# First q and k loads over all partitions from two queues, wider w_in packets, output blocks in score banks and a searched early order, in a fused attention and softplus-MLP kernel

## The chip, the cores and the metric

The kernel runs on one core of one Trainium2 chip. The metric is device microseconds of one execution. The profile also gives a span, from the first to the last instruction; it is some 2 us shorter than the time. Runs more than 1.5% above the fastest of the same kernel are called slow and are left out of all ratios.

The engines are named as in the profile: PE (matmul), PEld (weight load of PE), DVE (vector), ACT (scalar), POOL (GpSimd), SP (sync; it only issues transfers here). ACT issues transfers too, and ACTq and SPq mark the issuing itself.

## The reference, cut to what matters

```python
# q, k, v: (4, 8, 768, 64) f32     w_in: (512, 2048) f32     w_out: (2048, 512) f32
scores = q @ k.T / sqrt(64) - slope[h] * dist          # per batch and head
keep   = (key is one of the first 8) | (0 <= query - key < 96)
a      = softmax(where(keep, scores, -1e9))
x      = (a @ v), heads side by side                    # (4 * 768, 512)
g      = max(x @ w_in, 0) + log1p(exp(-abs(x @ w_in)))  # softplus
out    = g @ w_out                                      # (3072, 512) f32
```

A query needs only its own block of 128 keys, the block before and the 8 global ones. There are 4 sequences of 6 blocks, so 24 blocks of 128 tokens, and 12 groups of two blocks for the MLP. Inputs are f32; the kernel casts them to bf16.

## The kernel before

A planner inside the kernel lists every operation with an engine, a guessed duration and a rank, simulates the engines, and fixes each engine's order of instructions from that. On the chip each engine keeps to its order: an operation whose data are late holds up all that stand behind it.

```python
FIRST_UNITS = [[0], [1], [2, 3]]      # which sequences' first blocks are loaded together
FIRST_LOADS = "u0 u1 u2 i0 i1 i2 i3 i4 i5 i6 i7 o0 u3 o1 o2 o3 o4 o5 o6 o7".split()
FILLERS = 90                          # matmuls on zeros that keep PE busy at the start
O_KEYS = {(0, 1): ("s", 3), (1, 0): ("s", 2)}   # output banks other than "o"
...
s_ps = ps.tile([P, 16, P], F32, name="s_ps")    # ONE tile over four PSUM banks, for scores
x_ps = ps.tile([P, 512], F32, name="x_ps")      # one bank each
h_ps = [ps.tile([P, 512], F32, name=f"h_ps{i}") for i in range(2)]
o_ps = ps.tile([P, 512], F32, name="o_ps")
```

`u` is a unit of q, k and v, `i` an eighth of w_in (512 KB), `o` an eighth of w_out (512 KB). A first block's q comes in two halves, each to 64 partitions, as runs of two rows of 64 floats, which is 512 bytes.

```python
for y in range(2):
    eng = second if y else "SP"
    part = src[s, 4 * y : 4 * y + 4, sl, :]     # four heads, 128 rows
    def fn(part=part, slot=slot, y=y, eng=eng, nh=nh):
        return dma_on[eng].dma_start(
            raw_t[slot][64 * y : 64 * y + 64, 0 : P * nh].rearrange("p (h c) -> p h c", h=nh),
            part.rearrange("h (p r) d -> p h (r d)", r=2),
        )
```

w_in comes as eight column slices, in runs of 256 floats (1 KB); every weight is cast on POOL. q and k of the first blocks are cast and turned by PE into score banks, then copied out. Most output blocks accumulate 16 w_out matmuls in the one bank `o_ps` and are copied out by DVE:

```python
def store(g, ns, rank):
    parts = [(0, DM)] if 2 * g + ns < NIT - 1 else [(0, 256), (256, DM)]
    for a, z in parts:
        def cp(a=a, z=z):
            nc.vector.tensor_copy(osb[:, a:z], bank(key)[:, a:z])
    ...
```

The softmax here doesn't subtract the row's maximum and nothing guards it: scores larger than these inputs give would overflow.

## Time and profile before

| | before |
|---|---|
| time, median of the first 3 runs | 234.69 us (234.14 to 236.62) |
| span, mean granted clock | 232.6 us, 0.989 |
| PE / ACT / DVE / POOL busy | 92 / 67 / 49 / 42% |
| first w_in matmul | 21.17 us |
| third MLP group begins (129th w_in weight load) | 56.6 us |
| last w_in cast begins, last w_out cast begins | 30.3 us, 48.8 us |

The page of the kernel before, its head. The rows under the busy times cut the span into 40 equal slices: the granted PE clock in tenths, the busy share of the 16 DMA engines in tenths, and what they moved. The last line is the head of the chain of waits, as shares of the span.

```profile
span 232.6 us, 5037 instructions
PE 214.6 (92%) x1994; PEld 149.0 (64%) x2026; DVE 113.1 (49%) x219; ACT 154.9 (67%) x202; POOL 98.1 (42%) x178
PEclk9999999999998899999999999999999999999998
DMA  5999999999796449868877545899679422110021
GB/s 156 224 235 350 352 305 375 360 253 223 199 270 168 122 93 239 190 187 216 133 166 163 133 135 119 243 131 242 168 188 176 113 73 68 48 45 36 10 93 45
PE 78%; DMA 7%; DVE 4%; POOL 3%; issue 3%; ACT 3%; DVEq 0%; POOLq 0%; ACTq 0%
```

The windows view of the same kernel: stretch, length, then busy time and count of PE, PEld, DVE, ACT and POOL, the granted clock, the DMA share and GB/s. The share adds up packet times, so it can pass 1.

```profile
4.00:6.00 2.00, 2.00 (x14) 1.44 (x12) 1.69 (x8) 1.64 (x3) 0.00 (x0) 1.00 1.03 275
12.00:14.00 2.00, 0.94 (x12) 0.80 (x12) 0.62 (x2) 0.77 (x2) 0.00 (x0) 1.00 1.22 217
22.00:24.00 2.00, 1.73 (x21) 1.33 (x22) 0.74 (x3) 1.19 (x3) 1.48 (x2) 1.00 1.10 348
```

While q, k and v come, full engines move between 275 GB/s (4 to 6 us) and 217 (12 to 14 us); while w_in comes (22 to 24 us) they move 348.

The timeline of the kernel before: start, length, engine, line, operation, output and input with sizes, count, and in brackets the engine's idle time just before with what ended it. First the start-up, then the last output blocks.

```profile
5.70 0.43 DVE L370 CAST qb<-raw 128x512 bf16<-128x512 f32 x1
19.41 1.04 POOL L350 CAST w_in_bf<-raw 128x1024 bf16<-128x1024 f32 x1
21.17 1.05 PE L657 MATMUL h_ps<-XT,w_in_bf 128*128 128x256 bf16 x8
...
220.75 3.61 PE L704 MATMUL o_ps<-w_out_bf,g 128*128 128x512 bf16 x16 [0.78 <-DVE osb L728]
225.15 3.61 PE L704 MATMUL o_ps<-w_out_bf,g 128*128 128x512 bf16 x16 [0.78 <-DVE osb L728]
```

The first 21 us hold no MLP work. At the end PE stands still for 0.78 us before each of the last two output blocks, because the one bank has to be copied out first.

How far the needed work has come is read by counting the weight loads in the trace: every w_in and every w_out matmul has one, 768 and 384 in all. By the durations in the chain of waits (eight w_in matmuls 0.87 us, four w_out matmuls 0.86 us), one w_in load stands for 0.109 us of needed PE time and one w_out load for 0.215 us. All "needed work" below is an estimate from these two.

### The profile page before, as it was taken

Reading aid. Unit: us, or ns where it says so; the run is one execution under the profiler, and the core shown is the slowest. Engines: PE = TensorE matmul, PEld = TensorE weight load, DVE = VectorE, ACT = ScalarE, POOL = GpSimd, SP = SyncE. Lnnn points to the kernel's source line nnn. Section 1 sums busy time; section 2 is a strip of 40 time slices with the busy share of each in tenths; the row PEclk is TensorE's granted clock in tenths of the full one; section 3 lists DMA queues with packets and bytes.
Section 4 is the critical chain, followed back from the end, with each engine's and each line's share of the span. In section 5 each row is a group of like instructions: output and inputs, shape, how many; then the busy total and the mean of one; then the engine's idle time right before and its main releaser. Section 6 shows DMA issues by size and latency. Waiting matters only on the chain.

```text
span 232.6 us, 5037 instructions
## 1 busy us (share of the span) xinstructions
PE 214.6 (92%) x1994; PEld 149.0 (64%) x2026; DVE 113.1 (49%) x219; ACT 154.9 (67%) x202; POOL 98.1 (42%) x178
## 2 busy tenths in 40 slices
PE   8979889898995998999999999999999999999883
PEld 5758777555753476777667667676766867667531
DVE  5567315474179494059538448732944862111111
ACT  2432977751985259898878959876885987676600
POOL 3437645789456224767701606341573630000000
PEclk9999999999998899999999999999999999999998
DMA  5999999999796449868877545899679422110021
GB/s 156 224 235 350 352 305 375 360 253 223 199 270 168 122 93 239 190 187 216 133 166 163 133 135 119 243 131 242 168 188 176 113 73 68 48 45 36 10 93 45
DMA packets 76872, 40.97 MB, mean 176 GB/s; under 512 B 30640, under 2 KB 71856, under 8 KB 76848
## 3 DMA queue, kind: packets, MB, share of 16 engines
q1 hardware_dynamic: 75216, 39.86, 68.2%
q10 hardware_dynamic: 1632, 0.79, 1.4%
q8 instruction: 16, 0.26, 0.5%
q14 instruction: 8, 0.07, 0.1%
HBM read 27.26 MB, written 6.29 MB: 144 GB/s over the span
## 4 chain that ended last, share of the span: by engine, by line
PE 78%; DMA 7%; DVE 4%; POOL 3%; issue 3%; ACT 3%; DVEq 0%; POOLq 0%; ACTq 0%
PE o_ps L704 30%; PE h_ps L657 29%; PE s_ps L546 5%; PE h_ps L807 5%; DMA raw<-in_k_dram 4%; PE s_ps L704 3%; DMA raw<-in_v_dram 3%; PE x_ps L601 2%; ACT pb L581 2%; PE x_ps L598 2%; DVE z L572 2%; POOL vb L501 2%; POOL vb L395 1%; DVE osb L728 1%; PE s_ps L443 1%
## 5 line engine op out<-in xcount | busy, mean ns | idle before, releaser
L657 PE MATMUL h_ps<-XT,w_in_bf 128*128 128x256 bf16 x768 | 95.5, 273 | 1.5 <-POOL w_in_bf L350 0.9
L704 PE MATMUL o_ps<-w_out_bf,g 128*128 128x512 bf16 x323 | 84.8, 385 | 4.0 <-DVE osb L728 1.6
L657 PEld LDWEIGHTS <-w_in_bf 128*128 128x128 bf16 x768 | 73.2, 98 | 20.2 <-POOL w_in_bf L350 2.2
L672 ACT ACTIVATE e<-h_ps 128x512 f32<-128x512 f32 x96 | 59.9, 630 | 30.9 <-PE h_ps L657 30.3
L704 PEld LDWEIGHTS <-g 128*128 128x128 bf16 x384 | 35.9, 99 | 36.2 <-issue 7.0
L572 DVE TENSOR_TENSOR z<-s_ps,biasA 128x1024 f32<-128x1024 f32 x40 | 48.1, 1218 | 18.7 <-PE s_ps L546 17.0
L581 ACT ACTIVATE pb<-z 128x1024 bf16<-128x1024 f32 x40 | 41.8, 1050 | 18.9 <-DVE z L572 18.8
L683 ACT ACTIVATE g<-e 128x1024 bf16<-128x1024 f32 x48 | 50.7, 1056 | 1.3
L395 POOL CAST vb<-raw 64x512 bf16<-64x512 f32 (+1 forms) x60 | 32.8, 547 | 23.1 <-DMA raw<-in_v_dram 17.5
L728 DVE COPY osb<-o_ps 128x512 f32<-128x512 f32 (+1 forms) x23 | 15.2, 665 | 51.4 <-PE o_ps L704 51.3
L395 POOL CAST kb<-raw 64x512 bf16<-64x512 f32 (+1 forms) x44 | 24.0, 545 | 17.5 <-DMA raw<-in_k_dram 15.9
L501 POOL COPY vb<-vb 4x512 bf16<-4x512 bf16 x32 | 19.5, 610 | 17.1 <-PE x_ps L601 16.0
L611 DVE TENSOR_TENSOR xs<-x_ps,rcp 128x256 bf16<-128x256 f32 x46 | 19.5, 424 | 1.6
L610 DVE RECIPROCAL rcp<-x_ps 128x4 f32<-128x4 f32 x46 | 8.3, 179 | 22.8 <-PE x_ps L601 19.5
L601 PE MATMUL x_ps<-vb,pb 128*128 128x65 bf16 x160 | 15.1, 194 | 1.6 <-POOL vb L501 1.5
L598 PE MATMUL x_ps<-vb,pb 128*128 128x65 bf16 x160 | 15.5, 194 | 0.7 <-ACT g L683 0.7
L598 PEld LDWEIGHTS <-pb 128*128 128x128 bf16 x160 | 12.5, 98 | 5.2 <-issue 1.9
L492 POOL COPY kT<-kTf 128x32 bf16<-128x32 bf16 x16 | 3.5, 217 | 27.9 <-PE s_ps L546 27.0
L807 PE MATMUL h_ps<-blank 128*128 128x256 bf16 x90 | 13.8, 305 | 1.2 <-POOL blank L751 1.1
L546 PE MATMUL s_ps<-qT,kT 64*128 64x128 bf16 x288 | 13.4, 217 | 0.7 <-DVE z L572 0.7
L601 PEld LDWEIGHTS <-pb 128*128 128x128 bf16 x160 | 11.3, 97 | 3.4 <-issue 1.0
L370 DVE CAST qb<-raw 128x1024 bf16<-128x1024 f32 (+1 forms) x15 | 9.6, 641 | 7.5 <-DMA raw<-in_q_dram 7.5
(49 smaller groups left out, 98.6 us busy)
## 6 DMA issues: line engine op xcount, KB each, us to landing
out_dram<-osb SPq DMA_DIRECT2D x23, 256.0 KB, 2.4
raw<-in_moe_w_in_dram SPq DMA_DIRECT2D x8, 512.0 KB, 9.5
raw<-in_moe_w_out_dram SPq DMA_DIRECT2D x8, 512.0 KB, 8.3
raw<-in_q_dram SPq DMA_DIRECT2D x8, 512.0 KB, 4.3
raw<-in_k_dram SPq DMA_DIRECT2D x8, 512.0 KB, 5.5
raw<-in_v_dram SPq DMA_DIRECT2D x8, 512.0 KB, 4.9
raw<-in_q_dram SPq DMA_DIRECT2D x10, 128.0 KB, 3.5
raw<-in_k_dram SPq DMA_DIRECT2D x10, 128.0 KB, 3.6
```

The costliest lines, as they stand in the source:

```text
L395: copy_on[eng](dst, src[64 * x : 64 * x + 64, r, :, :])
L501: nc.gpsimd.tensor_copy(vb_of(prev)[sl, :, 0:D], vb_of(first)[sl, :, 0:D])
L546: nc.tensor.matmul(s_ps[:, reg, :].rearrange("p (r t) -> p r t", r=2), kt[rows, m, :], qv(rows, m), start=not biased, stop=True, skip_grou ...
L572: nc.vector.tensor_tensor(z[:, 0:nr, :], src, bias, ALU.add)
L581: nc.scalar.activation(pb[:, 0:nr, :], src, AF.Exp, scale=1.0 / root_d)
L598: nc.tensor.matmul(xv[:, m, :], pb[:, 2 * m, :], vb_of(n)[:, h, :], start=True, stop=False)
L601: nc.tensor.matmul(xv[:, m, :], pb[:, 2 * m + 1, :], vb_of(prev)[:, h, :], start=False, stop=True)
L657: last = nc.tensor.matmul(hv[:, j, :], w_in_bf[:, m, fb * P : fb * P + P], XT[g % NXG][:, m, :], start=(m == 0), stop=(m == NM - 1),)
L672: nc.scalar.activation(e[:, p % 2, :, :].rearrange("p j (b t r) -> p (j b) r t", b=2, r=2), hb[:].rearrange("p (a r t) -> p a r t", a=4, r=2),
L683: nc.scalar.activation(gt[:, 2 * p - 2 : 2 * p + 2, :].rearrange("p a t -> p (a t)"), e[:].rearrange("p a j t -> p (a j t)"), AF.Ln, bias=1.0,
L704: nc.tensor.matmul(bank(key), gt[:, fb, ns * P : ns * P + P], w_out_bf[:, fb, :], start=(fb == 0), stop=(fb == NFB - 1),)
L807: nc.tensor.matmul(h_ps[0][:, 0:256], blank[:, 0:P], blank[:])
```

## The change

The intent: get the first q and k sooner, start the MLP sooner, and shorten the tail.

```diff
-FIRST_UNITS = [[0], [1], [2, 3]]
-FIRST_LOADS = "u0 u1 u2 i0 i1 i2 i3 i4 i5 i6 i7 o0 u3 o1 o2 o3 o4 o5 o6 o7".split()
+FIRST_UNITS = [[0, 1], [2, 3]]
+FIRST_LOADS = "k0 q0 v0 q1 k1 i3 i1 i0 i2 v1 i7 i4 i5 i6 k2 o0 q2 o1 v2 o5 o7 o4 o2 o6 o3".split()
+ACT_LOADS = "q0 q1 k1 v0 k0".split()
+LEADS = {3: 1.75, 4: 2.5, 5: 2.5, 6: 2.5, 7: 3.25, 8: 2.75, ...}
+RANK = {0: -4, 1: -4, 2: -12, 3: 0, 4: 12, 5: 990, 6: -12, ...}
-O_KEYS = {(0, 1): ("s", 3), (1, 0): ("s", 2)}
+O_KEYS = {(0, 1): ("s", 3), (1, 0): ("s", 2),
+          (10, 0): ("s", 0), (10, 1): ("s", 1), (11, 0): ("s", 2), (11, 1): ("s", 3)}
+NARROW = (0, 1, 2)     # quarters of w_in that still come in 1 KB runs; the last comes in 2 KB runs
+ENG = {...}            # casts and copies of the first units on POOL, ACT, DVE
+ENG_W = {"i0": "POOL", "i1": "ACT", "i2": "POOL", ...}   # weight casts on three engines
...
 # in load_unit, first q and k: four rows of 64 floats are one run of 1 KB
+    for y in range(2):
+        eng = second if y else "SP"
+        c0 = 256 * (len(u) * y + x)
+        def fn(src=src, raw=raw, y=y, eng=eng, s_=s_, c0=c0):
+            return dma_on[eng].dma_start(
+                raw[:, c0 : c0 + 256],
+                src[s_, y::2, sl, :].rearrange("h (p r) d -> h p (r d)", r=4),
+            )
+        work = (0.38, 51.0)      # planned: 0.38 us of the engines for 128 KB
...
 # in store, the last block
-        parts = [(0, DM)] if 2 * g + ns < NIT - 1 else [(0, 256), (256, DM)]
+        parts = [(0, 256, "DVE", "SP"), (256, DM, "ACT", "ACT")] if last else [(0, DM, "DVE", "SP")]
```

Cut: the casts and copies that unpack the new layout, a shorter way to compute the distances, the later start of the second set of biases, and small changes of planned durations.

A first load now takes 4 heads of 32 four-row runs, 128 KB, to 128 partitions (head and run together make the partition). Units 0 and 1 together need 16 such loads for q and k: 2 MB.

## The prediction

> **What bounds the kernel now.** The page gives a span of 232.6 us (clock 0.989), PE 92% busy, but not all of that is needed work. In the chain eight w_in matmuls (128x256) take 0.87 us and four w_out matmuls (128x512) 0.86 us: 768 of the first need 84 us, 384 of the second 82 us; attention about 1.1 us of PE per block, 24 blocks. Needed: some 190 us. Busy times by stretch and line show where the other 40 go:
> - 0 to 21 us: no w_in matmul; PE runs 90 fillers and waits for the first blocks. First q cast at 5.7 us, first w_in cast at 19.4, first w_in matmul at 21.2. DMA moves about 220 GB/s while q, k, v come, 350 once w_in (1 KB runs) flows.
> - 21 to 55 us: each w_in matmul group waits for a weight cast that waits for its transfer (one per 1.5 us). By 55 us PE has done about 131 w_in and 41 w_out weight loads of 768 and 384. The third group begins at about 55 us.
> - 55 to 85 us: lumpy, a 6.7 us wait for v on the chain, the clock at half for 3.4 us near 75 us.
> - 85 to 220 us: PE-bound, needed work near 100%.
> - 220 to 232.6 us: two gaps of 0.78 us (w_out matmuls wait for the copy out of the only output bank), then 3.8 us of copy and store.
>
> **What the change does.** q and k of two first blocks at a time come in 1 KB runs over 128 partitions from two queues; by these rates 512 KB take 1.5 us instead of 2.3. (The Trainium skill, "DMA: Bandwidth & Descriptors", Specifications, puts line rate at 512 B and more; this trace differs, 220 against 350 GB/s, though start-up is in the 220.) w_in comes before v of the second pair. Only the last quarter of w_in uses 2 KB runs: worth 0.3 us. Weight casts spread from POOL (1.04 us each) over DVE, ACT and POOL; the first biases leave ACT (1.7 us).  The last four output blocks get score banks, and the last copy is split over DVE and ACT.
>
> **Cost on the critical path**, estimated from those durations:
> - The first 2.6 MB land by about 12 us, so the first w_in matmul comes at 16 to 17 us instead of 21.2; the last w_in lands at 26 instead of 30 us, all w_out at 42 instead of 48.
> - The third group starts at about 47 us instead of 55, with the first two groups' w_out work nearly done rather than two thirds (23 matmuls, 5 us). Together 13 us.
> - 55 to 85 us: 3 us of waits and low clock.
> - Tail: 2 x 0.78 plus about 0.4: 2 us.
> - Steady state: nothing.
> Sum 18 to 19 us: time about 216 us, range 208 to 226. Faster by over 2% 0.94, within 2% 0.05, slower 0.01.
>
> **What shows it right or wrong.** First w_in matmul at 16 to 17 us, first w_in cast near 14; DMA near 300 GB/s from 3 us on; third group's w_in matmuls by 47 us; output copies no longer release PE after 200 us; matmul counts per us from 100 to 200 us as before. Clock 0.99 or above.
>
> **What would make it wrong.** The order is fixed by a planner; a transfer later than planned blocks all behind it on its engine (ACT now has v casts ahead of its exponentials), and the 13 us shrink. The interleaved q layout gives PE strided operands: perhaps a microsecond or two. And 1 KB runs may be no faster when two queues share the engines.

## The result, and the profile after

| | before | changed |
|---|---|---|
| time, median of 4 runs | 234.84 us (234.14 to 236.62) | 247.08 us (244.89 to 248.29) |
| span, clock (profiled run) | 232.6 us, 0.989 | 245.2 us, 0.965 |
| first w_in matmul | 21.17 us | 38.85 us |
| 129th w_in weight load | 56.6 us | 74.7 us |

The ratio is 1.050, with a 95% interval of 1.041 to 1.059: slower by 5%, where 8% faster had been predicted. A ratio here is the mean time of one kernel's fast runs over that of the other's of the same rounds, so it is not quite the ratio of the medians.

The page of the changed kernel, the same lines:

```profile
span 245.2 us, 5044 instructions
PE 219.5 (90%) x1995; PEld 151.3 (62%) x2026; DVE 114.9 (47%) x219; ACT 159.5 (65%) x210; POOL 90.1 (37%) x166
PEclk9988756999999999999999999999999999999999
DMA  1527879999796876999992974479942761200112
GB/s 51 151 92 212 223 204 312 330 371 338 194 208 190 197 155 189 246 218 228 213 177 67 222 190 105 131 186 267 262 81 46 193 110 43 65 14 31 43 45 86
PE 69%; DMA 17%; DVE 7%; issue 2%; POOL 2%; ACT 1%; ACTq 1%; DVEq 0%
```

DMA has gone from 7 to 17% of the chain. In the third slice, where the kernel before has full DMA engines and 235 GB/s, this one has a share of 0.2 and 92 GB/s. The windows view of the changed kernel, in the order of its columns above:

```profile
4.00:6.00 2.00, 2.00 (x12) 1.36 (x10) 0.55 (x4) 0.00 (x0) 1.79 (x4) 1.00 0.27 93
14.00:16.00 2.00, 0.00 (x0) 0.00 (x0) 0.00 (x0) 0.00 (x0) 0.00 (x0) 1.00 0.28 88
15.00:40.00 25.00, 14.61 (x115) 10.06 (x117) 6.34 (x21) 9.13 (x17) 7.75 (x10) 0.68 0.74 206
30.00:35.00 5.00, 2.43 (x23) 1.75 (x20) 0.87 (x4) 1.67 (x3) 1.04 (x1) 0.50 0.61 157
```

From 14 to 16 us no compute engine does anything at all, and the transfers run at 88 GB/s with the engines a quarter busy. The longest pieces of the chain of waits of the changed kernel (start, length, what) say what the program waited for:

```profile
2.45 10.83 DMA raw<-in_q_dram
13.30 4.91 DMA raw<-in_q_dram
18.23 13.85 DMA raw<-in_k_dram
```

These three pieces alone are 29.6 us of loads of the first q and k. The timeline of the changed kernel, the start-up and the tail:

```profile
10.38 1.04 POOL L427 CAST kb<-raw 128x1024 bf16<-128x1024 f32 x1 [4.19 <-DMA raw<-in_k_dram]
25.12 1.04 POOL L427 CAST qb<-raw 128x1024 bf16<-128x1024 f32 x1 [6.78 <-DMA raw<-in_q_dram]
31.55 1.04 POOL L406 CAST w_in_bf<-raw 128x1024 bf16<-128x1024 f32 x1 [5.39 <-DMA raw<-in_moe_w_in_dram]
38.85 1.89 PE L742 MATMUL h_ps<-XT,w_in_bf 128*128 128x256 bf16 x8
...
230.13 3.61 PE L789 MATMUL s_ps<-w_out_bf,g 128*128 128x512 bf16 x15 [0.78 <-DVE osb L814]
234.53 3.61 PE L789 MATMUL s_ps<-w_out_bf,g 128*128 128x512 bf16 x16 [0.78 <-DVE osb L814]
238.93 2.75 PE L789 MATMUL s_ps<-w_out_bf,g 128*128 128x512 bf16 x12 [0.78 <-DVE osb L814]
241.72 0.42 DVE L814 COPY osb<-s_ps 128x256 f32<-128x256 f32 x1 [2.84 <-PE s_ps L789]
242.17 0.37 ACT L814 COPY osb<-s_ps 128x256 f32<-128x256 f32 x1 [12.79 <-DVE osb L814]
```

Two surprises. The casts of the first q and k wait for their transfers, the last of q until 25.12 us and the last of k, on ACT, until 32.23 us. And the tail, meant to lose its gaps, has three of 0.78 us instead of two, though each of the last four blocks has a bank of its own; the last ACT copy waits until the DVE copy beside it is done.

Weight loads done, w_in / w_out, counted in the four traces (sixteen-engines and split-tail are experiments below):

| by | before | changed | sixteen-engines | split-tail |
|---|---|---|---|---|
| 31 us | 56 / 0 | 0 / 0 | 40 / 0 | 45 / 0 |
| 55 us | 128 / 40 | 88 / 6 | 128 / 34 | 128 / 41 |
| 100 us | 287 / 112 | 228 / 92 | 304 / 118 | 306 / 120 |
| 200 us | 683 / 304 | 631 / 280 | 688 / 312 | 703 / 316 |

By 55 us the changed kernel is behind by 40 w_in and 34 w_out loads: 40 x 0.109 + 34 x 0.215, an estimated 11.7 us. By 200 us it is behind by 52 and 24, an estimated 10.8 us. So the loss is made in the start-up and kept; the spans differ by 12.6 us, and the third gap adds 0.8.

### The profile page after: what moved, and what is told of

It is laid out like the page before. It is cut to its first block, busy times and chain, and to the rows that moved or that the text cites. A ratio compares the mean times of both kernels' runs of the same rounds, so it can differ in the third digit from the quotient of the medians.

```text
span 245.2 us, 5044 instructions
## 1 busy us (share of the span) xinstructions
PE 219.5 (90%) x1995; PEld 151.3 (62%) x2026; DVE 114.9 (47%) x219; ACT 159.5 (65%) x210; POOL 90.1 (37%) x166
## 4 chain that ended last, share of the span: by engine, by line
PE 69%; DMA 17%; DVE 7%; issue 2%; POOL 2%; ACT 1%; ACTq 1%; DVEq 0%
PE h_ps L742 30%; PE o_ps L789 21%; DMA raw<-in_q_dram 9%; PE s_ps L789 9%; DMA raw<-in_k_dram 6%; PE s_ps L628 4%; DMA kT<-kb 2%; DVE z L657 2%; PE x_ps L683 2%; PE x_ps L686 2%; DVE osb L814 1%; DVE xs L696 1%; POOL kb L468 1%; ACT pb L666 1%; DVE w_out_bf L406 1%
## 5 line engine op out<-in xcount | busy, mean ns | idle before, releaser
L742 PE MATMUL h_ps<-XT,w_in_bf 128*128 128x256 bf16 x768 | 97.3, 274 | 0.5 <-DVE rcp L695 0.4
L789 PE MATMUL o_ps<-w_out_bf,g 128*128 128x512 bf16 x263 | 69.7, 379 | 1.3
L468 POOL CAST vb<-raw 64x512 bf16<-64x512 f32 (+1 forms) x50 | 27.6, 552 | 8.7 <-DMA raw<-in_v_dram 6.7
L583 POOL COPY vb<-vb 4x512 bf16<-4x512 bf16 x32 | 20.3, 633 | 20.6 <-PE x_ps L686 19.6
L789 PE MATMUL s_ps<-w_out_bf,g 128*128 128x512 bf16 x92 | 22.8, 379 | 4.1 <-DVE osb L814 2.9
L814 DVE COPY osb<-o_ps 128x512 f32<-128x512 f32 x18 | 12.4, 688 | 28.0 <-PE o_ps L789 28.0
L891 PE MATMUL h_ps<-blank 128*128 128x256 bf16 x90 | 15.8, 342 | 1.1 <-POOL blank L836 1.1
L683 PEld LDWEIGHTS <-pb 128*128 128x128 bf16 x160 | 12.6, 98 | 3.1
L814 DVE COPY osb<-s_ps 128x512 f32<-128x512 f32 (+1 forms) x6 | 3.9, 647 | 22.2 <-PE s_ps L789 22.2
L891 PEld LDWEIGHTS <-blank 128*128 128x128 bf16 x90 | 10.5, 121 | 6.1 <-issue 1.9
```

The costliest lines, as they stand in the source:

```text
L468: copy_on[eng](dst, raw)
L583: nc.gpsimd.tensor_copy(vb_of(prev)[sl, :, 0:D], vb_of(first)[sl, :, 0:D])
L683: nc.tensor.matmul(xv[:, m, :], pb[:, 2 * m, :], vb_of(n)[:, h, :], start=True, stop=False)
L742: last = nc.tensor.matmul(hv[:, j, :], w_in_bf[:, m, fb * P : fb * P + P], XT[g % NXG][:, m, :], start=(m == 0), stop=(m == NM - 1),)
L789: nc.tensor.matmul(bank(key), gt[:, fb, ns * P : ns * P + P], w_out_bf[:, fb, :], start=(fb == 0), stop=(fb == NFB - 1),)
L891: nc.tensor.matmul(h_ps[0][:, 0:256], blank[:, 0:P], blank[:])
```

## The experiments

**The theory.** The new source is written with the heads outermost, `h p (r d)`, and there are four heads in a load. The Trainium skill, "DMA: Bandwidth & Descriptors", section "Why a DMA increments its semaphore by 16 and not by 1", says that the number of engines of a transfer is the largest number up to 16 that divides the size of the slowest dimension (other than 1) of both access patterns. With 4 outermost on one side and 128 on the other that is 4 of 16 engines. The trace agrees: the share stands at 0.27 from 4 to 6 us, though by 4.2 us both queues had issued eight of these loads, 1 MB, and the last of them landed at 13.28 us; it is 0.28 from 14 to 16 us. I had not looked this section up for the prediction.

**The rivals.** First, that two queues hamper each other, which the prediction named as its risk. Second, that the granted clock, 0.50 from 30 to 35 us, is the cause and not a consequence. Third, later, that 1 KB runs matter at all.

### Sixteen engines

The row runs go outermost, so that partition p holds run p//4 of head p%4, and the unpacking follows. All else is as in the changed kernel.

```diff
-  src[s_, y::2, sl, :].rearrange("h (p r) d -> h p (r d)", r=4),
+  src[s_, y::2, sl, :].rearrange("h (p r) d -> p h (r d)", r=4),
...
-  v6 = t[:, 4 * x : 4 * x + 4, :].rearrange("p (a r) (m g) -> p m r g a", r=2, m=NPAIR)
+  v6 = t[:, 4 * x : 4 * x + 4, :].rearrange("p (a r) (g m) -> p m r g a", r=2, m=NPAIR)
...
-  cols = tr[:, 4 * x : 4 * x + 4, :].rearrange("p (a r) (m g) -> p r m g a", r=2, m=NPAIR)[:, r]
+  cols = tr[:, 4 * x : 4 * x + 4, :].rearrange("p (a r) (g m) -> p r m g a", r=2, m=NPAIR)[:, r]
```

> The changed kernel with one thing altered: each 128 KB load of the first q and k lists its 1 KB runs row group by row group (outermost source dimension 32) instead of head by head (outermost 4). Same bytes, same run size, same queues, same order on every engine. Theory (each of these loads ran on 4 of the 16 DMA engines): DMA share in the first 4 to 6 us goes from 0.27 to about 1.0 and 93 GB/s to 300 or more, the first w_in matmul comes at 16 to 18 us instead of 38.9, the granted clock stays above 0.98, time 214 to 221 us. Rival A (1 KB runs from two queues get in each other's way) and rival B (the searched order with strict engine queues is what blocks): both say no change, 244 to 248 us.

Measured: 232.35 us (231.19 to 233.74), ratio to before 0.993 (0.984 to 1.002); the result is correct. Against the changed kernel's 247.08 us that is 14.7 us gained by exchanging two dimensions (and by nothing else, as the unpacking does the same work). The windows view of this kernel:

```profile
4.00:6.00 2.00, 2.00 (x13) 1.48 (x11) 0.54 (x3) 0.74 (x1) 1.79 (x4) 1.00 0.87 242
```

The share is 0.87 in place of 0.27, and 242 GB/s in place of 93. First w_in matmul at 24.07 us in place of 38.85. What follows: the loads were the loss. But the kernel is then only level with before: the 214 to 221 us expected were missed, as was the matmul at 16 to 18 us, so the gain that was predicted is still missing.

### Eight engines

The source has all 8 heads outermost and half the rows. It fetches other rows than the casts expect, so its values are wrong; size, run length and queues are the same. (The comparison with the reference nevertheless passed, so that check is blind to this kind of mix-up and proves little for it.)

```diff
-  src[s_, y::2, sl, :].rearrange("h (p r) d -> h p (r d)", r=4),
+  src[s_, :, 64 * y : 64 * y + 64, :].rearrange("h (p r) d -> h p (r d)", r=4),
```

> Wrong result on purpose: the same bytes of the first q and k in 1 KB runs, but each load takes all 8 heads of half the rows, so the outermost source dimension is 8. Theory: 8 of 16 engines, DMA share about 0.5 to 0.55 and 180 GB/s while only q and k flow, first w_in matmul at 22 to 25 us, time 222 to 230 us, between the other two. Rivals A and B: as the changed kernel, 244 to 248 us.

Measured: 236.74 us (235.3 to 241.89, of which the last was a slow run and is left out of the ratio), ratio 1.010 (1.000 to 1.019); first w_in matmul at 27.6 us. Both lie between the other two kernels, as the theory wants, but above the 222 to 230 and 22 to 25 us expected. The windows view of this kernel:

```profile
4.00:6.00 2.00, 2.00 (x18) 1.60 (x16) 0.14 (x2) 0.00 (x0) 1.58 (x3) 1.00 0.51 175
```

With 4, 8 and 32 outermost (4, 8 and 16 engines by the rule) the share goes 0.27, 0.51, 0.87. The 2 MB of q and k would take, as an estimate from the measured rates, 22.5 us at 93 GB/s, 12.0 us at 175 and 8.7 us at 242. The steps between these, 10.5 and 3.3 us, stand beside the steps between the medians, 10.3 (247.08 to 236.74) and 4.4 us (236.74 to 232.35). So the number of engines alone accounts for the loss of the changed kernel.

### Warm clock

Every filler matmul of the changed kernel is done three times, to hold the clock up while PE waits.

```diff
-            nc.tensor.matmul(h_ps[0][:, 0:256], blank[:, 0:P], blank[:])
+            for _ in range(3):
+                nc.tensor.matmul(h_ps[0][:, 0:256], blank[:, 0:P], blank[:])
```

> The changed kernel with each filler matmul issued three times, so that PE stays busy and its clock full while it waits. Rival C (the half clock up to 40 us is the main loss): 232 to 238 us. Theory of the few engines: the clock goes above 0.98 but q still lands at 16 us and the first w_in matmul stays at 36 us or later; gain 1 to 4 us, time 243 to 246 us.

Measured: 250.89 us (250.35 to 251.35), ratio 1.072 (1.064 to 1.080). The windows view of this kernel:

```profile
15.00:40.00 25.00, 22.81 (x237) 19.43 (x236) 5.76 (x16) 8.09 (x14) 8.29 (x11) 1.00 0.74 209
```

The clock is 1.00 where the changed kernel had 0.68, at the same DMA rate (209 against 206 GB/s), and the time is worse, and worse than both expectations. So a full clock doesn't win the loss back. What the low clock cost by itself this run can't show, because the added fillers got in the way: up to 45 us they make up 68.5% of the chain of waits, the first transposes of k begin at 18.18 us instead of 11.47, and the first w_in matmul comes at 41.4 us instead of 38.85. That the low clock was a consequence is shown by the sixteen-engine kernel: with no filler added, its granted clock was 1.00. The Trainium skill, "TensorE: Matmul & The Clock Gate", section "Part 1: The HAM clock gate", has PE at half rate after an idle window of some 3.4 us. The trace of the changed kernel agrees: after PE had stood still for 3.97 us (to 17.16) the clock was 0.50 from 18 to 20 us, and after 3.23 us (to 26.21) it was 0.50 from 28 to 40 us; in the warm-clock kernel, with PE kept busy, it was 1.00.

### One queue

The sixteen-engine kernel, with all its first loads issued by SP.

```diff
-ACT_LOADS = "q0 q1 k1 v0 k0".split()
+ACT_LOADS = []
```

> As e1_sixteen, but all first loads are issued from the SP queue alone (the plan shifts with it). Rival A: faster than e1_sixteen by 2 us or more. Theory: the two queues only save issue time; each issue takes about 0.65 us for 128 KB on one queue, about 200 GB/s, so first w_in matmul 4 to 6 us later than in e1_sixteen and 3 to 6 us slower in time.

Measured: 236.19 us (235.06 to 237.58), ratio 1.011 (1.002 to 1.021): 3.8 us slower than with two queues. The first w_in matmul came at 25.7 us, 1.6 us later, where 4 to 6 us had been expected. The windows view of this kernel, then its timeline of issues:

```profile
4.00:6.00 2.00, 2.00 (x14) 1.52 (x12) 0.14 (x2) 0.00 (x0) 1.74 (x4) 1.00 0.67 190
0.72 2.59 SPq L368 DMA_DIRECT2D raw<-in_k_dram  x4
```

Four issues take 2.59 us, 0.65 us each. At 128 KB an issue, one queue can ask for no more than an estimated 202 GB/s, and 190 were moved. The rival that two queues are in each other's way is false: with one queue the rate falls, because the issuing is then the limit. How much of the 3.8 us is that isn't shown, since the plan shifts with the queues, and a shifted plan alone can move as much (see the replanned kernel below). The Trainium skill, "DMA: Bandwidth & Descriptors", section "Issuing engines are not separate DMA queues", says that issuing from several engines saves only the sequencer's time, "which is usually small relative to the DMA itself". The kind of saving agrees; for 128 KB loads it was not small here.

### Score banks as two tiles

This and the next two ran together. The sixteen-engine kernel's timeline has a strange order at the first scores:

```profile
14.35 0.60 ACT L666 ACTIVATE pb<-s_ps 128x512 bf16<-128x512 f32 x1
15.00 0.61 PE L522 MATMUL s_ps<-ident,qb 128*128 128x128 bf16 x8 [0.31 <-ACT pb L666]
15.64 0.60 ACT L666 ACTIVATE pb<-s_ps 128x512 bf16<-128x512 f32 x1 [0.69 <-PE s_ps L522]
```

PE's transposes wait for an exponential, and the next exponential waits for the transposes, though they use different banks of `s_ps`. The theory: waits are placed for a whole tile, not for a bank. The rival: some true dependence on data. In the experiment the four banks become two tiles of two banks, with nothing else changed:

```diff
-    s_ps = ps.tile([P, 16, P], F32, name="s_ps")
+    s_ab = [ps.tile([P, 8, P], F32, name=f"s_ps{i}") for i in range(2)]
+    def s_reg(r0, nr):
+        return s_ab[r0 // 8][:, r0 % 8 : r0 % 8 + nr, :]
...  # every s_ps[:, a:b, :] becomes s_reg(a, b - a)
```

> e1_sixteen with the four score banks declared as two tiles of two banks instead of one tile of four; same plan, same order. In the e1_sixteen trace the second exponential of the first block (0.60 us at 15.64) waits for the transposes of the next q, which write other banks, and these had waited for the first exponential. Theory D (waits are placed per tile, so banks that the plan thinks free are not): these waits go, the first w_in matmul comes at 20 to 22 us instead of 24.1, time 224 to 229 us. Rival E (what is left of the missing gain is the transfers alone, 250 GB/s for the first 14 us and few transfers in flight): first w_in matmul within 1 us of 24.1, time 230 to 234 us.

Measured: 230.28 us (228.48 to 231.07), ratio 0.981 (0.974 to 0.989); first w_in matmul at 20.9 us in place of 24.07. The timeline of this kernel, at the start and in the tail:

```profile
13.46 1.09 ACT L670 ACTIVATE pb<-s_ps 128x512 bf16<-128x512 f32 x2
14.09 0.61 PE L526 MATMUL s_ps<-ident,qb 128*128 128x128 bf16 x8
212.56 7.07 PE L793 MATMUL s_ps<-w_out_bf,g 128*128 128x512 bf16 x32 [0.78 <-DVE osb L818]
220.41 2.75 PE L793 MATMUL s_ps<-w_out_bf,g 128*128 128x512 bf16 x12 [0.78 <-DVE osb L818]
```

The two exponentials now follow each other at once (x2 in 1.09 us), with the transposes beside them. The first w_in matmul is where the theory wanted it; the time is not, it lies at the edge of what the rival of the transfers foretold (230 to 234 us), and the sixteen-engine kernel ran in another call. In the tail, PE goes from block (10, 1) in bank 1 to block (11, 0) in bank 2, which is another tile, with no gap (x32 in 7.07 us); the block changes inside one tile keep their 0.78 us. The theory holds, and it explains why the changed kernel's tail, where all four blocks are in one tile, had three gaps.

### Kernel before, score banks as two tiles

The same edit on the kernel before.

> The kernel before with the same two tiles and nothing else. Theory D: before pays such waits too, but its plan was weaker, 229 to 233 us. Rival E: 233 to 236 us.

Measured: 234.79 us (233.89 to 235.76), ratio 1.003 (0.994 to 1.011). No gain, where the theory had expected 229 to 233 us. The waits do go here too: in the kernel before the first two exponentials start at 11.57 and 13.17 us, with the split they follow each other from 11.11 us, and the third group begins at 55.2 us instead of 56.6. Why nothing of it is left at the end stays open.

### Split tail

The two-tile kernel, with the last four output blocks in four different tiles.

```diff
     (10, 0): ("s", 0),
-    (10, 1): ("s", 1),
-    (11, 0): ("s", 2),
-    (11, 1): ("s", 3),
+    (10, 1): ("s", 2),
+    (11, 0): ("x",),
+    (11, 1): ("o",),
```

> e7_split with the last four output blocks in four different tiles (two score tiles, x bank, o bank). In the changed kernel PE waits 0.78 us three times near the end for the copy of another bank of the same tile. Theory D: these three gaps go, 2.3 us less than e7_split (1.8 to 2.8). If waits went by bank and the gaps had another cause: no difference from e7_split beyond 0.5 us.

Measured: 227.7 us (227.42 to 228.89), ratio 0.972 (0.966 to 0.979). This version beats both kernels. The timeline of its tail:

```profile
215.04 3.62 PE L793 MATMUL x_ps<-w_out_bf,g 128*128 128x512 bf16 x16
218.49 3.62 PE L793 MATMUL o_ps<-w_out_bf,g 128*128 128x512 bf16 x16
```

No idle time stands before either block. Two gaps of 0.78 us are gone against the two-tile kernel; the medians differ by 2.6 us and the spans of the profiled runs by 1.1 us (226.7 and 225.6), so the 1.6 us of the gaps is within what was seen, and the rest isn't explained (other banks can also shift the plan).

### 512-byte runs

The split-tail kernel with its first q and k in runs of 512 bytes. Rows are mixed up; the bytes and the 16 engines are the same.

```diff
-    raw[:, c0 : c0 + 256],
-    src[s_, y::2, sl, :].rearrange("h (p r) d -> p h (r d)", r=4),
+    raw[:, c0 : c0 + 256].rearrange("p (a c) -> p a c", a=2),
+    src[s_, y::2, sl, :].rearrange("h (p r) d -> p h (r d)", r=2),
```

> Wrong values on purpose: e9_split_tail with the first q and k read in 512-byte runs instead of 1 KB, into the same 128 partitions, on all 16 engines, same order. The step under test is the prediction's '512 KB take 1.5 us instead of 2.3 us' for 2 MB in all, 3.2 us of transfer. If run size is what sets 220 against 350 GB/s: DMA near 220 GB/s from 3 to 10 us, first w_in matmul 2 to 3 us later, time 2 to 3 us more than e9_split_tail. If the start is limited elsewhere (issue, landings of transfers in flight): within 1 us.

Measured: 228.3 us (228.01 to 228.88), ratio 0.974 (0.969 to 0.980). That is 0.6 us above the split-tail kernel. It was run at another time. The windows view of the split-tail kernel and then of this one:

```profile
4.00:6.00 2.00, 2.00 (x16) 1.61 (x14) 0.15 (x2) 0.00 (x0) 1.62 (x5) 1.00 0.92 297
4.00:6.00 2.00, 2.00 (x16) 1.60 (x14) 0.54 (x4) 0.00 (x0) 1.80 (x4) 1.00 0.96 270
```

The rate falls a little, the first w_in matmul comes at 24.2 us instead of 22.0, and almost none of it reaches the end. The run length, on which the prediction had built its first sum, is worth less than 1 us.

### Plain leads and ranks

The split-tail kernel without the searched tables.

```diff
-LEADS = {3: 1.75, 4: 2.5, ...}
-RANK = {0: -4, 1: -4, 2: -12, ...}
+LEADS = {}
+RANK = {}
```

> e9_split_tail with the searched load leads and block ranks taken away (every unit 2.5 groups ahead and every block at its plain rank, as in the kernel before). Between 55 and 100 us the kernel before falls back by another 5 us of needed PE work and e9_split_tail by none. If the searched leads and ranks are what removed that: 3 to 5 us more than e9_split_tail, lost between 55 and 100 us. If it came from the early order or from other moves: within 1.5 us.

Measured: 227.46 us (227.18 to 227.88), ratio 0.971 (0.966 to 0.976). The same time as with the tables: these two parts of the search gained nothing here.

### Replanned with measured transfer times

The planner had 0.38 us for 128 KB, which is 345 GB/s; the traces of the sixteen-engine kernels show less. Here it gets times nearer to the measured ones.

```diff
-    work = (0.38, 51.0)
+    work = (0.48, 51.0)
...
-    work = (0.5, 33.0)
+    work = (0.62, 33.0)
```

> e9_split_tail with the planner told the measured early rates (about 0.48 us for 128 KB of q or k and 0.62 us for 128 KB of v instead of 0.38 and 0.50), so that the fixed order of the engines fits the landings. If the late first w_in matmul (22.0 us in e9_split_tail, 17 us forecast) comes mostly from work queued in strict order behind landings later than planned: first w_in matmul at 19 to 20.5 us and 1 to 3 us less time than e9_split_tail. If the bytes themselves are the limit (7 MB of q, k, v and w_in by 30.9 us in both before and e9_split_tail): within 1 us of e9_split_tail's 227.7.

Measured: 232.55 us (231.65 to 234.82), ratio 0.992 (0.985 to 0.998): 4.9 us worse. The first w_in matmul is unchanged (22.1 us). The chain of waits of this kernel has two long waits for k:

```profile
61.97 5.72 DMA raw<-in_k_dram
103.92 6.46 DMA raw<-in_k_dram
```

They are not the cause by themselves: the chain of the split-tail kernel has two such waits for k as well, 4.59 us from 62.02 and 5.52 us from 97.68. By the counts this kernel is level at 55 us (128 / 43), an estimated 3.4 us behind at 100 us (291 / 112) and 7.4 us at 200 us (667 / 300); its profiled run was the longest of the five. So a truer number for the first loads shifted the planned order long after them, to a worse one; which operations lost the time stays open. A miss on both expectations, and a warning: a change anywhere in the plan can move 5 us.

### First group before the second pair

The split-tail kernel, with the plan pushed to do the first MLP group before the attention of blocks 2 and 3.

```diff
-RANK = {0: -4, 1: -4, 2: -12, 3: 0, ...}
+RANK = {0: -4, 1: -4, 2: 990, 3: 990, ...}
...
-    work = (0.38, 51.0)
+    work = (2.0 if (which, i) in (("k", 1), ("q", 1)) else 0.38, 51.0)
```

> e9_split_tail with the plan made to believe that the second pair's q and k land late, and with the second pair's attention ranked behind the first group's w_in matmuls, so that PE does not stand in line behind k (its cast was at 16.3 us in e9_split_tail) before the transposes that the first group needs. If the first w_in matmul at 22.0 us is set by this line: 19 to 20.5 us and 0.5 to 2 us less time than e9_split_tail's 227.7. If the weights' arrival is what counts (last w_in cast at 30.9 us whatever the order): first w_in matmul may move, time within 1 us.

Measured: 237.66 us (235.67 to 237.88), ratio 1.013 (1.006 to 1.021): worse by 10 us. The first w_in matmul came later (24.6 us) and the third group at 63.9 us. Neither of the two expectations held; why the order is so much worse wasn't followed up.

### Kernel before, tail in two tiles

The kernel before, with the last blocks of the last two groups in `x_ps`.

```diff
-O_KEYS = {(0, 1): ("s", 3), (1, 0): ("s", 2)}
+O_KEYS = {(0, 1): ("s", 3), (1, 0): ("s", 2), (10, 1): ("x",), (11, 1): ("x",)}
```

> The kernel before with nothing changed but that the last four output blocks alternate between the o bank and the free x bank, two tiles. Theory D: the two 0.78 us waits of PE at 220.0 and 224.4 us go, 1.3 to 1.8 us less than the kernel before. If the gap is inherent to a change of block: no difference beyond noise of 0.7 us.

Measured: 234.66 us (233.6 to 236.68), ratio 1.002 (0.995 to 1.010). The timeline of its last two output blocks:

```profile
221.97 3.62 PE L704 MATMUL o_ps<-w_out_bf,g 128*128 128x512 bf16 x16
225.42 3.62 PE L704 MATMUL x_ps<-w_out_bf,g 128*128 128x512 bf16 x16
```

The blocks start 3.45 us apart; in the kernel before it was 4.40 us. So the gaps are gone, and yet the time is the same: by 85 us this kernel had done 192 w_in loads where before had 198, with 96 w_out loads in both. The edit also moved the plan, and the gain was lost to that or to the scatter of the kernel before; which of the two stays open. Inconclusive for the time, clear for the gaps.

## Why the prediction was wrong

Predicted were 216 us (208 to 226) and 0.94 for faster; measured were 247.08 us. Point by point:

- **"q and k of two first blocks at a time come in 1 KB runs over 128 partitions from two queues; by these rates 512 KB take 1.5 us instead of 2.3."** This is the step that failed. The rates were read from transfers that used all engines. The new loads ran on 4 of 16: 93 GB/s, an estimated 5.6 us for 512 KB. I looked at run length and partitions and not at the outermost dimension of the source. It is shown by the 4, 8 and 16 engine runs, and it accounts for the whole loss.
- **"First w_in matmul at 16 to 17 us", third group "at about 47 us", "together 13 us".** Measured: 38.85 and 74.7 us. With all engines at work the matmul comes at 24.07 us, with the tiles split too at 20.9 to 22 us, which is no sooner than before; and the third group at 57.8 us (split-tail) against 56.6 us before. So this part was wrong even without the four engines. The reason is in the bytes: before the last w_in cast can start, 3 MB of q, k and v and 4 MB of w_in must land, in both kernels; that cast starts at 30.3 us before and at 30.87 us in the split-tail kernel (29.2 to 31.8 us in the other two-queue kernels with 16 engines). In the chain of waits of the latter, 10.79 and 8.04 us before that cast are waits for w_in. Reordering loads within the same bytes moved no end, and the average rate did not rise.
- **"This trace differs, 220 against 350 GB/s."** The Trainium skill, "DMA: Bandwidth & Descriptors", section "Specifications", puts line rate at 512 bytes and more. In the kernel before, full engines moved 217 to 275 GB/s in 512-byte runs against 348 in 1 KB runs, but those loads also differ in their partitions and sizes. Where only the run length was changed, it was 270 against 297 GB/s, 1.1 times as fast and not the 1.5 times of the prediction's sum (some loads of v, in short runs in both, lie in that stretch), and less than 1 us of time hung on it.
- **"The last four output blocks get score banks", tail 2 us.** Reading was right that the gaps cost 0.78 us each; wrong was that four banks are four places. They are one tile, and the waits go by tile: three gaps instead of two. In four tiles the gaps go.
- **"The last copy is split over DVE and ACT."** The copies ran one after the other, 241.72 and 242.17 us. Both read one bank, and both write one tile, `osb`. The Trainium skill, "PSUM — Partial Sum Buffer", section "PSUM bank collisions raise a hardware error", counts ScalarE reading beside VectorE in the same bank and quadrant as a collision, to be guarded by bank. The trace agrees that they were kept apart, with 0.03 us between them. Whether the bank or the wait by tile did it isn't separated; that two banks would let them overlap, no run here shows.
- **"55 to 85 us: 3 us of waits and low clock."** Not seen in the changed kernel: from 55 to 100 us it does 140 w_in and 86 w_out loads, 33.8 us of needed work, against 32.8 before. Once the loads are mended the size is about right: 37.2 us in the sixteen-engine kernel and 36.4 in the split-tail one, so about 4 us gained. It doesn't come from the searched leads and ranks (227.46 us without them), and the replanned kernel lost it (32.6). Which part of the new order brings it stays open.
- **"Steady state: nothing."** Right. From 100 to 200 us before does 396 w_in and 192 w_out loads, the changed kernel 403 and 188: 84.4 and 84.3 us of needed work.
- **"Clock 0.99 or above."** It was 0.965; a consequence of the late loads, since the sixteen-engine kernel had 1.00.
- **The named risks.** "A transfer later than planned blocks all behind it" did happen, only far more strongly. "1 KB runs may be no faster when two queues share the engines" did not: one queue alone was 3.8 us slower, in a shifted plan. Strided operands: no run measured them alone.

Where the split-tail kernel's 7.1 us over before come from, as an estimate from the counts: 3.6 us of needed work between 55 and 100 us, 1.0 us between 100 and 200 us (397 and 196 loads, 85.4 us, against 84.4), and 1.6 us of gaps at the end; nothing before 55 us, where 128 / 41 stand against 128 / 40. That is 6.2 us; the rest isn't accounted for.

## What to carry to other kernels

Before costing a transfer by its bytes and run length, look at the size of the outermost dimension of both its sides: a share of the DMA engines that stands at a quarter or a half with loads still queued is a sign that most engines have no part in it (loads issued too slowly lower the share as well, here to 0.67). Before counting on an earlier end of a start-up, look whether fewer bytes stand before its last transfer or the rate rises: here another order of the same 7 MB ended at about the same time. And a bank is free only if the program's waits know it as a thing of its own: give buffers that should overlap separate tiles.

## What the Trainium skill lacked or had wrong

- "DMA: Bandwidth & Descriptors", the number of engines of a transfer: right (4, 8 and 32 outermost, so 4, 8 and 16 engines, gave shares of 0.27, 0.51 and 0.87, and 93, 175 and 242 GB/s), but it doesn't say how this looks in a profile, namely a share that stays near k/16 while transfers are queued.
- "DMA: Bandwidth & Descriptors", Specifications: line rate from 512 bytes. In the kernel before, 512-byte runs of q, k and v moved 217 to 275 GB/s with the engines full (shares of 1.22 and 1.03), and 1 KB runs of w_in 348 GB/s (share 1.10); with nothing changed but the run length it was 270 against 297 GB/s. So 1 KB was somewhat faster than 512 bytes here, by much less than the first pair of numbers suggests.
- "DMA: Bandwidth & Descriptors", on issuing engines: the saved issue time is "usually small". Here an issue of 128 KB takes 0.65 us, one queue moved 190 GB/s at a share of 0.67 where two moved 242 at 0.87, and the time with one was 3.8 us longer (in a shifted plan).
- "PSUM — Partial Sum Buffer" gives the rule by bank, and no page says that the waits of a program built this way go by PSUM tile: 0.78 us between two output blocks in two banks of one tile, none between blocks in two tiles.
